# Running sums of squares for the next batch: accumulating DMAs in place of VectorE additions

## The chip, the cores and the metric

The kernel runs on one core of a Trainium2 chip. The metric is the device time of one execution in microseconds (us); the time of a kernel is the median of its runs. The engines of the core are TensorE (PE, matrix products; PEld is its loading of weights), VectorE (DVE), ScalarE (ACT), GpSimd (POOL), and SyncE (SP), which here only issues transfers. Each engine works through its own instructions in their order and waits on semaphores where it needs what another engine, or a transfer, has made.

## What is computed

Two layers follow one another: an attention between channels, for 4 batches of 6016 rows and 256 channels, and a gated feed-forward layer for all 24064 rows.

```python
# B, N, C = 4, 6016, 256; d_ff = 1536; float32 in and out
qn = q / (norm(q, axis=1) + 1e-6)          # norms over the 6016 rows, one for each channel
kn = k / (norm(k, axis=1) + 1e-6)
s  = kn.transpose(0, 2, 1) @ qn / tau      # 256 x 256 for each batch
a  = softmax(s)
x  = (v @ a).reshape(B * N, C)
out = (sigmoid(x @ w_gate) * (x @ w_val)) @ w_out
```

The norms need, for each batch, the sum over all rows of the squares of q and of k. Those sums are what the change touches.

## The kernel before

The kernel folds the attention of a batch into the two weights of the feed-forward layer (the tiles gh_G and gh_H), so that a batch then runs as 12 pieces of up to 512 rows, each with 12 steps over d_ff. A step ("slot") is one gate product, one value product, a tanh on ScalarE and a multiplication on VectorE; the output products of the piece before are strewn between them. 4 x 12 x 12 = 576 slots make up nearly all of the time. While batch b runs through its slots, the scores, squares and norms of batch b+1 are computed beside it, as side work tied to slots.

The pools whose sizes matter:

```python
qkpool = pool("qkpool", 5)      # q and k tiles
sqpool = pool("sqpool", 2)      # squares, two buffers for q and two for k
mpool = pool("mpool", 2)
opool = pool("opool", 2)        # output rows
psg = pool("psg", 2, space=PSUM)   # ps_gate
psv = pool("psv", 2, space=PSUM)   # ps_val
```

The sums of squares: ScalarE squares four rows of each partition at a time (128 partitions x 4 x 256), the squares are added into the accumulator acc (one for q, w = 0, and one for k, w = 1), two halvings on VectorE fold the four columns of acc into one, and TensorE sums over the partitions.

```python
def acc_square(b, g, w):
    t0, nt = groups[g]
    src = qk[b, t0][w]
    acc = st[b]["acc"][w]
    st[b]["sq", w] = squares(b, t0, nt, w, nc.scalar, acc if g == 0 else None)

def acc_add(b, g, w):
    t0, nt = groups[g]
    if g == 0:
        return
    acc = st[b]["acc"][w]
    nc.vector.tensor_tensor(
        out=acc[:, :nt, :], in0=acc[:, :nt, :], in1=st[b]["sq", w][:, :nt, :], op=ALU.add
    )

def acc_fold(b, w):
    acc = st[b]["acc"][w]
    for n in (2, 1):
        nc.vector.tensor_tensor(out=acc[:, :n, :], in0=acc[:, :n, :], in1=acc[:, n : 2 * n, :], op=ALU.add)
```

The slots at which this side work stands (FC is 12, groups has 12 entries, the last one with 3 rows of a partition instead of 4):

```python
first, last = (14 if b == 0 else 0), 8 * FC
for g, (t0, nt) in enumerate(groups):
    s0 = first + g * (last - first) // NCH
    # ... loads of q and k, score products
    for w in range(2):
        at(s0 + 1 + 4 * w, acc_square, n, g, w)
        slot = s0 + 3 + 4 * w
        at(slot + 2 if w == 0 and slot % FC == 8 else slot, acc_add, n, g, w)
# ...
s0 = 8 * FC + 2
at(s0 if b == 0 else s0 - 2, acc_fold, n, 0)
at(s0 + 1 if b == 0 else s0, acc_fold, n, 1)
at(s0 + 3, norms_mm, n)
```

One slot of the main work, and what GpSimd does for the output rows:

```python
def glu(b, ci, f, between=None):
    # ... PE: ps_gate and ps_val, two products each of 128x512
    nc.scalar.activation(out=g_sb[:, :n], in_=ps_gate[:, :n], func=ACT.Tanh, scale=0.5)
    nc.vector.scalar_tensor_tensor(
        out=hts[b, ci][:, f, :n], in0=g_sb[:, :n], scalar=1.0, in1=ps_val[:, :n],
        op0=ALU.add, op1=ALU.mult,
    )

def whole(p):
    o = out_tile(b, ci)
    nc.scalar.copy(o[:, p : p + half + 1 : half, :], states[p]["ps"].rearrange("p (t c) -> p t c", c=C))
    # ...
    add = nc.gpsimd.tensor_tensor
    add(out=ends, in0=ends, in1=states[p]["m"][:, 1:3, :], op=ALU.add)
    add(out=ends, in0=ends, in1=mids, op=ALU.subtract)
```

GpSimd also issues the loads of q, k and v, which turn float32 into bfloat16. Batch 0 has its squares summed in the opening stage by other lines, which the change does not touch.

Of the kernel before, what the change touches and what calls it, by code (L numbers as in the profile page):

```python
# [13 lines left out]
ALU = mybir.AluOpType  # L14
# [39 lines left out]
def kernel(  # L54
# [20 lines left out]
    nc = tc.nc  # L75
# [76 lines left out]
    t0, nt = groups0[0]  # L152
# [40 lines left out]
    for f0, nf in pieces:  # L193
        if f0 + nf == DFF:
            load_v(0, 1)
        for w, src in enumerate((moe_w_gate, moe_w_val)):
            nc.gpsimd.dma_start(
                out=w_sb[w][f0 // FG][:, :, ds(f0 % FG, nf)],
                in_=src.rearrange("(t p) f -> p t f", p=P)[:, :, ds(f0, nf)],
# [5 lines left out]
    for n in range(FC // TPC):  # L205
        w_f32[n] = f32pool.tile([P, TPC, C], FP32, tag="f32", name="w_f32")
        nc.gpsimd.dma_start(
            out=w_f32[n], in_=moe_w_out.rearrange("(t p) c -> p t c", p=P)[:, n * TPC : (n + 1) * TPC, :]
# [16 lines left out]
    st = {}  # L225
# [17 lines left out]
    def squares(b, t0, nt, which, engine, sq=None):  # L243
        src = qk[b, t0][which]
        if sq is None:
            sq = sqpool.tile([P, TPC, C], BF16, tag=f"sq{which}", name=f"sq{which}")
        if engine is nc.scalar:
            nc.scalar.activation(out=sq[:, :nt, :], in_=src[:, :nt, :], func=ACT.Square)  # L248
        else:
            engine.tensor_tensor(  # L250
                out=sq[:, :nt, :], in0=src[:, :nt, :], in1=src[:, :nt, :], op=ALU.mult
            )
        return sq
# [27 lines left out]
    def acc_add(b, g, w):  # L281
        t0, nt = groups[g]
        if g == 0:
            return
        acc = st[b]["acc"][w]
        nc.vector.tensor_tensor(  # L286
            out=acc[:, :nt, :], in0=acc[:, :nt, :], in1=st[b]["sq", w][:, :nt, :], op=ALU.add
        )

    def acc_fold(b, w):  # L290
        acc = st[b]["acc"][w]
# [405 lines left out]
    acc = st[0]["acc"]  # L697
    last0 = len(groups0) - 1
    adds, ends = [], []
    for g, (t0, nt) in enumerate(groups0):  # L700
# [5 lines left out]
        sq = [squares(0, t0, nt, w, engines[w], acc[w] if g == 0 else None) for w in range(2)]  # L706
        while adds:
            w, last_sq = adds.pop()
# [44 lines left out]
    def side_work(b):  # L753
# [24 lines left out]
        for g, (t0, nt) in enumerate(groups):  # L778
            s0 = first + g * (last - first) // NCH
            if b == 0:  # L780
                at(max(FC - 3, s0 - 12), load_qk, n, t0, nt)
            elif s0 >= 24:
                at(s0 - 24, load_qk, n, t0, nt)
            for u in range(nt):
                at(first + (t0 + u) * (last - first) // NT, score, n, t0, u)
            if g == 0:
                at(s0, acc_start, n)
# [4 lines that stand above are left out]
# [98 lines left out]
```

## Time and profile before

| What | Value |
|---|---|
| Time, median of 3 runs | 802.43 us (802.38 to 802.65) |
| Span of the profiled execution | 800.8 us |
| Granted TensorE clock | 0.998 of full speed |
| VectorE additions into acc (line 286) | 66, 58.9 us in all |
| Loads of v, 256 KB each, issue to landing | 5.2 us (median) |
| Share of the DMA engines' time, GpSimd's queue and SyncE's | 30.0% and 20.3% |

The profile has the busy time of each engine, the chain of waits that ended last, a row for each group of alike instructions (line, engine, operation, tiles, count, busy time, mean length, idle time before them and what ended it), and rows for transfers with the time from issue to landing. The time line of an engine gives, for each instruction, its start and its length in us, and in square brackets the idle time before it and what ended that. L128, L286 and so on are lines of the kernel.

### The profile page before, as it was taken

The numbers are of one execution on the slowest core, as the hardware profiler recorded it, in microseconds if no ns is written. First come the engines' busy times: TensorE is split into PE (matmuls) and PEld (weight loads), VectorE is DVE, ScalarE is ACT, GpSimd is POOL, SyncE is SP. The second block draws the span as 40 slices with busy tenths as digits, with TensorE's granted clock in tenths as the row PEclk, the third lists the DMA queues.
The fourth block names the chain that finished last, engine by engine and source line by source line (L and its number), as shares of the span: only waits on it lengthen the run. The fifth ranks groups of instructions, "written<-read, shape, count | busy, mean of one in ns | idle before, by whom it ended". The sixth has DMA issues, their size and how long they took to land.

```text
span 800.8 us, 17849 instructions
## 1 busy us (share of the span) xinstructions
PE 781.9 (98%) x6719; PEld 498.6 (62%) x6733; DVE 711.9 (89%) x1216; ACT 526.3 (66%) x887; POOL 359.8 (45%) x574
## 2 busy tenths in 40 slices
PE   4899999999999999999999999999999999999998
PEld 2556666666666666666666666666666566666666
DVE  5768999999979999999987999999998898998995
ACT  3766777765667777775667777776666566666664
POOL 4564545446443454335543544443544244444433
PEclk9999999999999999999999999999999999999999
DMA  9997757432765557422575477524323323423402
GB/s 214 205 194 132 132 98 139 89 67 53 139 120 105 93 114 128 85 53 55 111 127 106 96 124 119 99 54 93 66 55 87 66 54 78 82 54 77 76 28 74
DMA packets 79543, 78.89 MB, mean 99 GB/s; under 512 B 52064, under 2 KB 57312, under 8 KB 79456
## 3 DMA queue, kind: packets, MB, share of 16 engines
q0 software_dynamic: 22384, 39.60, 30.0%
q1 hardware_dynamic: 56496, 37.30, 20.3%
q8 instruction: 52, 0.85, 0.4%
q10 hardware_dynamic: 576, 0.85, 0.3%
q14 instruction: 35, 0.29, 0.1%
HBM read 79.04 MB, written 24.64 MB: 129 GB/s over the span
## 4 chain that ended last, share of the span: by engine, by line
PE 95%; DMA 3%; POOL 0%; issue 0%; DVE 0%; ACT 0%; POOLq 0%; DVEq 0%
PE ps_gate L128 30%; PE ps_val L128 30%; PE ps_o L128 28%; PE ps_s L128 4%; DMA k_sb<-in_k_dram 3%; PE ps_gh L128 2%; POOL q_sb L138 0%; PE ps_end L128 0%; POOL k_sb L138 0%; PE ps_n L128 0%; DVE x_sb L382 0%; PE ps_r L128 0%; ACT e_sb L400 0%; DVE y_sb L394 0%; POOL ident_f masks.py:199 0%
## 5 line engine op out<-in xcount | busy, mean ns | idle before, releaser
L520 ACT ACTIVATE g_sb<-ps_gate 128x512 f32<-128x512 f32 (+1 forms) x576 | 339.4, 590 | 224.7 <-PE ps_gate L128 213.9
L521 DVE SCALAR_TENSOR_TENSOR hT<-g_sb,ps_val 128x512 bf16<-128x512 f32 (+1 forms) x576 | 385.5, 671 | 70.0 <-ACT g_sb L520 59.5
L128 PE MATMUL ps_gate<-vT,gh_G 128*128 128x512 bf16 (+1 forms) x1152 | 337.6, 375 | 0.1
L128 PE MATMUL ps_val<-vT,gh_H 128*128 128x512 bf16 (+1 forms) x1152 | 337.5, 375 | 0.0
L543 DVE TENSOR_TENSOR sums<-hT 128x768 bf16<-128x768 bf16 (+1 forms) x460 | 282.0, 613 | 0.0
L128 PEld LDWEIGHTS <-sums 128*128 128x128 bf16 x2670 | 183.0, 98 | 81.9 <-DVE sums L543 0.5
L128 PEld LDWEIGHTS <-gh_H 128*128 128x128 bf16 x1152 | 112.7, 98 | 130.6 <-DVE gh_H L468 0.3
L614 POOL TENSOR_TENSOR out_sb<-out_sb,m_sb 128x256 f32<-128x256 f32 x89 | 78.2, 878 | 232.7 <-ACT out_sb L604 201.6
L128 PE MATMUL ps_o<-w_sums,sums 128*128 128x128 bf16 x1602 | 154.2, 219 | 0.0
L128 PEld LDWEIGHTS <-hT 128*128 128x128 bf16 x1200 | 88.3, 98 | 46.8
L598 POOL TENSOR_TENSOR m_sb<-m_sb 128x128 f32<-128x128 f32 x89 | 42.7, 479 | 149.9 <-ACT m_sb L597 149.8
L128 PEld LDWEIGHTS <-gh_G 128*128 128x128 bf16 x1152 | 96.6, 98 | 14.7 <-DVE gh_G L468 0.3
L128 PE MATMUL ps_o<-w_out_sb,sums 128*128 128x128 bf16 x1068 | 96.2, 219 | 0.0
L128 PE MATMUL ps_o<-w_sums,hT 128*128 128x128 bf16 x1068 | 95.5, 219 | 0.0
L128 PE MATMUL ps_s<-k_sb,q_sb 128*128 128x256 bf16 x376 | 70.5, 291 | 13.9 <-ACT k_sb L184 7.1
L615 POOL TENSOR_TENSOR out_sb<-out_sb 128x256 f32<-128x256 f32 x89 | 77.4, 870 | 7.0
L604 ACT COPY out_sb<-ps_o 128x512 f32<-128x512 f32 x89 | 52.3, 587 | 11.7 <-PE ps_o L128 9.4
L286 DVE TENSOR_TENSOR acc<-acc,sq 128x1024 bf16<-128x1024 bf16 (+1 forms) x66 | 58.9, 892 | 0.0
L599 POOL TENSOR_TENSOR m_sb<-m_sb 128x128 f32<-128x128 f32 x89 | 53.2, 598 | 7.0
L248 ACT ACTIVATE sq<-k_sb 128x1024 bf16<-128x1024 bf16 (+2 forms) x44 | 44.9, 1029 | 11.8 <-DMA k_sb<-in_k_dram 11.7
L128 PEld LDWEIGHTS <-q_sb 128*128 128x128 bf16 x376 | 33.5, 104 | 20.2 <-issue 9.5
L597 ACT COPY m_sb<-ps_o 128x384 f32<-128x384 f32 x89 | 42.7, 480 | 3.6 <-PE ps_o L128 1.0
(86 smaller groups left out, 306.6 us busy)
## 6 DMA issues: line engine op xcount, KB each, us to landing
out_dram<-out_sb SPq DMA_DIRECT2D x43, 512.0 KB, 3.4
v_sb<-in_v_dram POOLq DMA_DIRECT2D x44, 256.0 KB, 5.2
q_sb<-in_q_dram POOLq DMA_DIRECT2D x35, 256.0 KB, 4.4
k_sb<-in_k_dram POOLq DMA_DIRECT2D x35, 256.0 KB, 6.5
q_sb<-in_q_dram POOLq DMA_DIRECT2D x4, 512.0 KB, 11.6
k_sb<-in_k_dram POOLq DMA_DIRECT2D x4, 512.0 KB, 13.6
w_f<-in_moe_w_out_dram POOLq DMA_DIRECT2D x3, 512.0 KB, 9.4
out_dram<-out_sb SPq DMA_DIRECT2D x3, 384.0 KB, 2.8
```

What stands on the lines that cost most here:

```text
L128: nc.tensor.matmul(out, lhsT=lhsT, rhs=rhs, start=start, stop=stop, **kw)
L248: nc.scalar.activation(out=sq[:, :nt, :], in_=src[:, :nt, :], func=ACT.Square)
L286: nc.vector.tensor_tensor(out=acc[:, :nt, :], in0=acc[:, :nt, :], in1=st[b]["sq", w][:, :nt, :], op=ALU.add)
L520: nc.scalar.activation(out=g_sb[:, :n], in_=ps_gate[:, :n], func=ACT.Tanh, scale=0.5)
L521: nc.vector.scalar_tensor_tensor(out=hts[b, ci][:, f, :n], in0=g_sb[:, :n], scalar=1.0, in1=ps_val[:, :n], op0=ALU.add, op1=ALU.mult,)
L543: nc.vector.tensor_tensor(out=sums[b, ci, g][:, m, :, : half * P], in0=hT[:, f0 + k0 : f1 : 2, ds(r0 * half * P, half * P)], in1=hT[:, f0 ...
L597: nc.scalar.copy(m, states[p]["ps"][:, : 3 * P].rearrange("p (n c) -> p n c", c=P))
L598: nc.gpsimd.tensor_tensor(out=m[:, 1, :], in0=m[:, 1, :], in1=m[:, 2, :], op=ALU.add)
L599: nc.gpsimd.tensor_tensor(out=m[:, 2, :], in0=m[:, 1, :], in1=m[:, 0, :], op=ALU.add)
L604: nc.scalar.copy(o[:, p : p + half + 1 : half, :], states[p]["ps"].rearrange("p (t c) -> p t c", c=C),)
L614: add(out=ends, in0=ends, in1=states[p]["m"][:, 1:3, :], op=ALU.add)
L615: add(out=ends, in0=ends, in1=mids, op=ALU.subtract)
```

## The change

The additions of the squares into acc leave VectorE. Each becomes a transfer within the on-chip memory, issued from GpSimd's queue, which reads the squares and adds them into acc as it writes. The purpose is to take work off VectorE, which carries 89% of busy time. The fold, the squares and all slots stay as they are.

```diff
@@ acc_add
         if g == 0:
             return
         acc = st[b]["acc"][w]
-        nc.vector.tensor_tensor(
-            out=acc[:, :nt, :], in0=acc[:, :nt, :], in1=st[b]["sq", w][:, :nt, :], op=ALU.add
-        )
+        nc.gpsimd.dma_start(out=acc[:, :nt, :], in_=st[b]["sq", w][:, :nt, :], accum_op=ALU.add)
```

In the order of instructions that results, 66 additions go from VectorE and 66 transfers come to GpSimd's queue (22 for each of the batches 1, 2 and 3); no other instruction changes its place on any engine. Each transfer waits for its squares from ScalarE and for the transfer before it into the same accumulator, and the fold waits for the last of them.

## The prediction, made before the result was known

> **What bounds the kernel now.** I read the shares of busy time first, then the chain that ended last, then the rows of what the change touches.
>
> ```profile
> PE 781.9 (98%) x6719; PEld 498.6 (62%) x6733; DVE 711.9 (89%) x1216; ACT 526.3 (66%) x887; POOL 359.8 (45%) x574
> PE 95%; DMA 3%; POOL 0%; issue 0%; DVE 0%; ACT 0%; POOLq 0%; DVEq 0%
> L521 DVE SCALAR_TENSOR_TENSOR hT<-g_sb,ps_val 128x512 bf16<-128x512 f32 (+1 forms) x576 | 385.5, 671 | 70.0 <-ACT g_sb L520 59.5
> L286 DVE TENSOR_TENSOR acc<-acc,sq 128x1024 bf16<-128x1024 bf16 (+1 forms) x66 | 58.9, 892 | 0.0
> ```
>
> TensorE is busy for 98% of the span and is 95% of the chain; VectorE, which the change relieves, has 0% of the chain. Since a busy TensorE need not be one at its peak, I checked its rate. All its products together stream 1.807 million columns (the lengths of the moving operands summed over the trace). In the time line, back-to-back 128x512 products start every 0.215 us, so 512/0.215 = 2381 columns per us; 1.807 million at that pace is 759 us of the 800.8. The rest is nearly all in the opening: the list of waits has 13.9 us of TensorE waiting for the first q and k, all before the first slot. Adding up, from the starts of neighbouring products, what is over their columns gives 16.5 us in the first 40 us and then about 0.4 us in each 20 us, a little over 1 us only at the three changes of batch. The stretch table agrees (columns: stretch, its length, then PE, PEld, DVE, ACT, POOL busy with counts, clock, DMA share, GB/s):
>
> ```profile
> 340.00:360.00 20.00, 20.00 (x179) 12.88 (x177) 19.18 (x33) 14.43 (x25) 7.83 (x11) 1.00 0.25 53
> 660.00:680.00 20.00, 20.00 (x177) 12.49 (x176) 17.80 (x30) 11.99 (x22) 8.59 (x12) 1.00 0.31 71
> ```
>
> The first has side work, the second (last batch) has none. VectorE falls from 19.2 to 17.8, TensorE stays full in both. **There is almost nothing for a freer VectorE to win.** What can move the time is whether the change makes TensorE wait.
>
> [...] The trace shows GpSimd taking 0.57 us for a v load. [...] Here the smallest transfer from this queue (row<-rT, 0.5 KB) takes 2.7 us from issue to landing, so the measured 2.7 is used. [...] additions into acc take from 0.55 to 1.22 us, and the longer one shown below (1.08 us) lies beside GpSimd's additions. [...]
>
> **Part by part.**
>
> *Removed:* 66 x 0.892 = 58.9 us of VectorE, off the chain. Worth 0 to 1 us, from the rates above; I take 0.
>
> *Added on GpSimd:* 66 x 0.57 (the v load's) = 38 us; 45% busy becomes some 50%. Its waits are on ScalarE's copies (201.6 and 149.8 us in all), so this fits into its idle time.
>
> *Added on the DMA engines:* GpSimd's queue moved 22384 packets in 30.0% of 16 engines' span, so 0.30 x 16 x 800.8 / 22384 = 0.172 us for each. 66 x 128 rows = 8448 packets, at twice that (two reads, my choice) 8448 x 0.344 / 16 = 182 us, spread over some 490 us in which the engines are 25 to 60% busy. It fits.
>
> *The running chain:* a sum waits for the one before into the same acc. Squares of one w come 10.4 to 11.4 us apart (7.5 to 10.5 in batch 1). Landing in 5 to 7 us hides there.
>
> *The fold* is where the wait shows, for VectorE stands in the queue with main work behind it. Batch 2, on GpSimd, then on VectorE:
>
> ```profile
> 361.40 0.89 POOL L614 TENSOR_TENSOR out_sb<-out_sb,m_sb 128x256 f32<-128x256 f32 x1 [2.42 <-ACT out_sb L604]
> 362.36 0.93 POOL L615 TENSOR_TENSOR out_sb<-out_sb 128x256 f32<-128x256 f32 x1
> 363.23 0.57 POOL L148 DMA_DIRECT2D v_sb<-in_v_dram  x1
> ```
>
> ```profile
> 361.61 1.08 DVE L286 TENSOR_TENSOR acc<-acc,sq 128x768 bf16<-128x768 bf16 x1
> ...
> 365.54 0.75 DVE L293 TENSOR_TENSOR acc<-acc 128x512 bf16<-128x512 bf16 x2
> 366.20 0.68 DVE L521 SCALAR_TENSOR_TENSOR hT<-g_sb,ps_val 128x512 bf16<-128x512 f32 x1
> ```
>
> The last k addition (361.61) becomes a transfer. The new instruction order puts it on GpSimd behind the second pair of output additions, ahead of the v load: it is issued at 362.36 + 0.93 = 363.3, though its squares were ready at 358.5. The fold for k starts at 365.54, 2.2 us later. The hT behind it ends at 366.88, and the ps_val that reuses its bank starts on TensorE at 367.23:
>
> ```profile
> 367.23 0.59 PE L128 MATMUL ps_val<-vT,gh_H 128*128 128x512 bf16 x2
> ```
>
> 0.35 us of slack. **The landing time L** of this last transfer (three rows of 512 B in a partition, 192 KB) decides. Loads into 192 KB tiles land in 3.5 to 4.2 us, so 0.8 to 1.5 over the fixed 2.7. I double the 1.1 in the middle, since the accumulate reads two operands, and add 0.6 because a 512 KB output store is issued at 363.3 too: L = 2.7 + 2.2 + 0.6 = 5.5, an estimate. Landing at 368.8, fold to 369.5, hT to 370.1, TensorE late by 370.1 - 367.23 = 2.9.
>
> Batch 3 has the same pattern 192.7 us later: issue at 555.03 + 0.93 = 556.0, fold for k at 558.2, slack 0.36: late by 2.9. In batch 1 the slots differ by one, and the order puts the v load first: issue at 171.4, landing 176.9, where the fold began at 174.26 and the slack was 0.06: late by 2.4. The q folds are safe: issued at 166.1 (batch 1) against a fold at 172.2, and at 353.9 against 363.2.
>
> Sum: 2.4 + 2.9 + 2.9 = 8.2 us. Being full afterwards, TensorE never makes this up. 802.4 + 8.2 = 810.6; with half a us for stray delays, **811 us**.
>
> **Rivals.**
>
> 1. *Hidden anyway.* If the accumulate lands as a load does (L about 4.0), the delays are 0.9 + 1.4 + 1.4 = 3.7: about 806. For: no memory off the chip is touched. Against: the fixed 2.7 alone outlasts the 2.2 us between issue and fold, so nothing is hidden wholly.
> 2. *Slow accumulate.* If adding 16-bit elements runs at a quarter of a load's rate or less, L is 8 to 12. Each us of L costs 3 us: L = 8 gives about 819, L = 10 about 825. From about 10 us a second wait begins: the sums cannot keep pace with the squares, GpSimd stands blocked at its queue's head, output additions behind it come late, ScalarE's copies into m_sb and out_sb wait for buffers (two each), PSUM is not freed, and TensorE waits in every group of side work. That could reach 840 or more. The transfers would then also delay v loads. For: nothing in the profile has this rate. Against: nothing but that the casting loads keep 0.172 us a packet.
> 3. *VectorE was the bound.* It is 95% busy beside side work. If its additions held TensorE back, removing 58.9 us would bring some of it. Against: the full TensorE in both stretches, and the slack between hT and ps_val, which is small (0.06 to 1 us) but not negative.
>
> **Range and chances.** L from about 4 to 10 maps to 806 to 825; with stray gains and losses I give 804 to 826. 2% over 802.4 is 818.5, so an L of about 8.1. I put 0.29 on L beyond that or on a blocked queue, 0.01 on rival 3, and 0.70 on within 2%.
>
> **What would show it.** The row of additions at L286 gone from VectorE, its busy time down by 55 to 60 us, TensorE's nearly unchanged; a transfer row acc<-sq, x66, of 5 to 7 us to landing; among VectorE's waits a new one of the fold on that transfer, three times 2 to 4 us; new idle on TensorE just after each fold of k and nowhere else; the stretch between neighbouring folds as long as before (192.7 us) apart from it. The prediction is wrong if the span grows inside the groups before a fold (GpSimd blocked, rival 2), if GpSimd takes well over 0.57 us for an issue, if L is under 3.5 or over 9, or if the span shrinks.

## The result and the profile after

The changed kernel takes 809.17 us (median of 4 runs, 808.11 to 810.24) against 802.45 us before (median of 4 runs). The ratio is 1.0083, 95% interval 1.0065 to 1.0102: 6.7 us slower, within 2%, and close to the 811 predicted. The profiled execution has a span of 806.2 us against 800.8.

The page of the changed kernel: busy time by engine, the chain that ended last, then the main VectorE row, the row of the products into ps_val, the new row on GpSimd, and the new transfer with its median time from issue to landing.

```profile
PE 782.4 (97%) x6719; PEld 498.7 (62%) x6733; DVE 671.7 (83%) x1150; ACT 525.1 (65%) x887; POOL 415.7 (52%) x640
...
PE 92%; DMA 5%; POOL 1%; DVE 1%; issue 1%; ACT 0%; DVEq 0%; POOLq 0%
...
L519 DVE SCALAR_TENSOR_TENSOR hT<-g_sb,ps_val 128x512 bf16<-128x512 f32 (+1 forms) x576 | 387.8, 674 | 109.0 <-ACT g_sb L518 92.9
L128 PE MATMUL ps_val<-vT,gh_H 128*128 128x512 bf16 (+1 forms) x1152 | 337.5, 375 | 3.2 <-DVE hT L519 3.2
...
L286 POOL DMA_DIRECT2D acc<-sq x66 | 58.1, 881 | 6.5 <-ACT sq L248 1.9
...
acc<-sq POOLq DMA_DIRECT2D x60, 256.0 KB, 5.2
```

VectorE lost its row at L286 and 40 us of busy time; TensorE is as busy as before (782.4 against 781.9 us), in a longer span. What VectorE was spared turns up as its waiting for ScalarE: its idle time before hT grew from 70.0 to 109.0 us. The chain has larger shares for transfers (5%, from 3%) and for VectorE (1%, from 0%), and ps_val has 3.2 us of idle time that it did not have. Its row in the kernel before:

```profile
L128 PE MATMUL ps_val<-vT,gh_H 128*128 128x512 bf16 (+1 forms) x1152 | 337.5, 375 | 0.0
```

TensorE's list of waits in the changed kernel (who waited for whom, us in total, times, longest) says which:

```profile
PE ps_s L128 <- DMA k_sb<-in_k_dram: 6.9, 5, 2.1
PE ps_s L128 <- ACT k_sb L184: 6.9, 1, 6.9
PE ps_val L128 <- DVE hT L519: 3.2, 2, 1.6
PE ps_n L128 <- DVE acc L291: 2.3, 1, 2.3
```

The first two belong to the opening and were there before (6.8 and 7.1 us). The other three waits are new, 5.5 us together, which is the growth of the span (5.4). VectorE's list has their cause:

```profile
DVE acc L291 <- DMA acc<-sq: 7.2, 3, 2.8
```

Three folds of k, one for each of batches 1 to 3, wait for the last transfer into the accumulator. The time lines of batch 2 show one of them. GpSimd first, the instruction's start and length in us:

```profile
363.89 0.89 POOL L612 TENSOR_TENSOR out_sb<-out_sb,m_sb 128x256 f32<-128x256 f32 x1 [2.29 <-ACT out_sb L602]
364.86 0.73 POOL L613 TENSOR_TENSOR out_sb<-out_sb 128x256 f32<-128x256 f32 x1
365.53 0.86 POOL L286 DMA_DIRECT2D acc<-sq  x1
```

VectorE:

```profile
367.17 0.68 DVE L519 SCALAR_TENSOR_TENSOR hT<-g_sb,ps_val 128x512 bf16<-128x512 f32 x1
370.05 0.75 DVE L291 TENSOR_TENSOR acc<-acc 128x512 bf16<-128x512 bf16 x2 [2.20 <-DMA acc<-sq]
370.72 0.68 DVE L519 SCALAR_TENSOR_TENSOR hT<-g_sb,ps_val 128x512 bf16<-128x512 f32 x1
```

TensorE:

```profile
369.30 0.59 PE L128 MATMUL ps_gate<-vT,gh_G 128*128 128x512 bf16 x2
371.46 0.59 PE L128 MATMUL ps_val<-vT,gh_H 128*128 128x512 bf16 x2 [1.56 <-DVE hT L519]
```

The transfer is issued at 365.53, behind the output additions, and takes 4.4 us to land; the fold, ready since about 367.8, starts at 370.05; hT follows it at 370.72; TensorE, which needs the ps_val buffer that this hT reads, stands 1.56 us.

### The profile page after: what moved, and what is told of

Read it like the earlier page. It is cut to its first block, busy times and chain, and to the rows that moved or that the text cites. A ratio compares the mean times of both kernels' runs of the same rounds, so it can differ in the third digit from the quotient of the medians.

```text
span 806.2 us, 17947 instructions
## 1 busy us (share of the span) xinstructions
PE 782.4 (97%) x6719; PEld 498.7 (62%) x6733; DVE 671.7 (83%) x1150; ACT 525.1 (65%) x887; POOL 415.7 (52%) x640
## 3 DMA queue, kind: packets, MB, share of 16 engines
q0 software_dynamic: 31888, 56.51, 43.3%
## 4 chain that ended last, share of the span: by engine, by line
PE 92%; DMA 5%; POOL 1%; DVE 1%; issue 1%; ACT 0%; DVEq 0%; POOLq 0%
PE ps_val L128 29%; PE ps_gate L128 29%; PE ps_o L128 27%; PE ps_s L128 4%; DMA k_sb<-in_k_dram 3%; PE ps_gh L128 2%; DMA acc<-sq 2%; POOL out_sb L612 0%; ACT out_sb L602 0%; DVE acc L291 0%; POOL q_sb L138 0%; DVE hT L519 0%; PE ps_end L128 0%; POOL k_sb L138 0%; PE ps_n L128 0%
## 5 line engine op out<-in xcount | busy, mean ns | idle before, releaser
L519 DVE SCALAR_TENSOR_TENSOR hT<-g_sb,ps_val 128x512 bf16<-128x512 f32 (+1 forms) x576 | 387.8, 674 | 109.0 <-ACT g_sb L518 92.9
L541 DVE TENSOR_TENSOR sums<-hT 128x768 bf16<-128x768 bf16 (+1 forms) x460 | 285.7, 621 | 0.0
L612 POOL TENSOR_TENSOR out_sb<-out_sb,m_sb 128x256 f32<-128x256 f32 x89 | 83.9, 942 | 201.2 <-ACT out_sb L602 170.1
L596 POOL TENSOR_TENSOR m_sb<-m_sb 128x128 f32<-128x128 f32 x89 | 45.6, 513 | 123.1 <-ACT m_sb L595 122.9
L613 POOL TENSOR_TENSOR out_sb<-out_sb 128x256 f32<-128x256 f32 x89 | 67.4, 757 | 7.0
L286 POOL DMA_DIRECT2D acc<-sq x66 | 58.1, 881 | 6.5 <-ACT sq L248 1.9
L602 ACT COPY out_sb<-ps_o 128x512 f32<-128x512 f32 x89 | 52.1, 586 | 11.8 <-PE ps_o L128 9.5
L597 POOL TENSOR_TENSOR m_sb<-m_sb 128x128 f32<-128x128 f32 x89 | 54.7, 615 | 7.0
L248 ACT ACTIVATE sq<-k_sb 128x1024 bf16<-128x1024 bf16 (+2 forms) x44 | 44.8, 1027 | 12.0 <-DMA k_sb<-in_k_dram 11.8
```

The source lines that it names most:

```text
L286: nc.gpsimd.dma_start(out=acc[:, :nt, :], in_=st[b]["sq", w][:, :nt, :], accum_op=ALU.add)
L519: nc.vector.scalar_tensor_tensor(out=hts[b, ci][:, f, :n], in0=g_sb[:, :n], scalar=1.0, in1=ps_val[:, :n], op0=ALU.add, op1=ALU.mult,)
L541: nc.vector.tensor_tensor(out=sums[b, ci, g][:, m, :, : half * P], in0=hT[:, f0 + k0 : f1 : 2, ds(r0 * half * P, half * P)], in1=hT[:, f0 ...
L596: nc.gpsimd.tensor_tensor(out=m[:, 1, :], in0=m[:, 1, :], in1=m[:, 2, :], op=ALU.add)
L597: nc.gpsimd.tensor_tensor(out=m[:, 2, :], in0=m[:, 1, :], in1=m[:, 0, :], op=ALU.add)
```

## Experiments

The theory: the loss is three waits of the fold on the last k transfer of a batch, fixed by the distance between issue and fold; the other 63 transfers are hidden, and the relief of VectorE brings nothing. The rivals: the loss is spread over all 66 transfers (a longer GpSimd queue, traffic), or a gain from the relief hides inside it.

**Last group back on VectorE.**

```diff
+        if g == NCH - 1:
+            nc.vector.tensor_tensor(... acc + sq, as before ...)
+        else:
             nc.gpsimd.dma_start(..., accum_op=ALU.add)
```

> Undoes one part: only the additions of the last group (q and k, 6 in all) go back to VectorE, 60 of the 66 transfers stay. If the whole loss is the fold's wait for the last k transfer (my theory), TensorE no longer waits after the fold and the time is 802 to 803 us. If the loss is spread, by GpSimd's longer queue, by the transfers' traffic or by a lower clock, at least two thirds of it stay: 807 us or more.

Measured: 801.87 us (801.67 to 801.96), ratio to before 0.9993 (0.9984 to 1.0001). With 60 of the 66 transfers still in place, nothing of the loss is left.

**Only the last k addition as a transfer.**

```diff
+        if (g, w) != (NCH - 1, 1):
+            nc.vector.tensor_tensor(... acc + sq, as before ...)
+        else:
             nc.gpsimd.dma_start(..., accum_op=ALU.add)
```

> The mirror: only the last k addition of each batch (3 of 66) is an accumulating transfer, all others stay on VectorE. Theory: the loss is as large as with all 66, some 808 to 810 us. If the loss is spread over the 66 transfers: 803 us or less.

Measured: 809.8 us (808.89 to 810.82), ratio 1.0091 (1.0076 to 1.0106). Three transfers do what 66 do. VectorE's list of waits for this kernel has three waits of about the same sum (7.3 against 7.2 us), though not wait for wait (the longest is 3.4 us here, against 2.8):

```profile
DVE acc L296 <- DMA acc<-sq: 7.3, 3, 3.4
```

**The last k transfer earlier in GpSimd's queue.**

```diff
             for w in range(2):
                 at(s0 + 1 + 4 * w, acc_square, n, g, w)
                 slot = s0 + 3 + 4 * w
+                if (g, w) == (NCH - 1, 1):
+                    at(8 * FC - 2, acc_add, n, g, w)
+                    continue
```

> All 66 transfers stay, but the last k one is put one or two slots earlier in GpSimd's queue, so that it no longer stands behind the second pair of output additions (and, in batch 1, the v load). It can be issued when its squares are ready, some 4.3 us earlier in batches 2 and 3 and 3.5 us earlier in batch 1. Theory: it lands before the fold in batches 2 and 3 and about on time in batch 1, and the time is 802 to 803.5 us. If the wait is for GpSimd or for the number of transfers, the time stays at 807 or more.

Measured: 802.07 us (801.99 to 802.18), ratio 0.9995 (0.9987 to 1.0004). GpSimd's time line of this kernel has the transfer ahead of the second pair of output additions, instead of behind it:

```profile
358.88 0.86 POOL L286 DMA_DIRECT2D acc<-sq  x1
361.24 0.87 POOL L612 TENSOR_TENSOR out_sb<-out_sb,m_sb 128x256 f32<-128x256 f32 x1 [1.50 <-ACT out_sb L602]
```

VectorE's list of waits no longer has the fold. The transfer also lands faster: in 3.4, 3.0 and 3.6 us in batches 1 to 3, instead of 6.1, 4.4 and 4.5. It now runs ahead of the output store and the v load, which fits, but this run does not tell the two apart. All 66 transfers can be hidden, and then the kernel is as fast as before; that it is faster is not shown, since the interval has 1 in it.

**No additions at all.** The additions of groups 1 to 11 are left out; the norms of batches 1 to 3 are then those of the first group alone.

```diff
         if g == 0:
             return
         acc = st[b]["acc"][w]
-        nc.gpsimd.dma_start(out=acc[:, :nt, :], in_=st[b]["sq", w][:, :nt, :], accum_op=ALU.add)
+        return
```

> The additions of groups 1 to 11 are left out altogether (the norms of batches 1 to 3 then use the first group alone, so part of the computation is missing): VectorE has its 58.9 us less and nothing takes their place. Theory: TensorE was full already, so 802 to 802.5 us, the same as before within 0.1%. If VectorE had held TensorE back: 795 to 800 us.

Measured: 802.44 us, ratio 0.9999 (0.9990 to 1.0008). Taking the 58.9 us of additions from VectorE with nothing in their place is worth nothing, so the relief had nothing to give.

**The fold one slot later.**

```diff
-        at(s0 + 1 if b == 0 else s0, acc_fold, n, 1)
-        at(s0 + 3, norms_mm, n)
-        at(s0 + 4, root_seed, n)
-        at(s0 + 4, root_steps, n)
+        at(s0 + 2 if b == 0 else s0 + 1, acc_fold, n, 1)
+        at(s0 + 4, norms_mm, n)
+        at(s0 + 5, root_seed, n)
+        at(s0 + 5, root_steps, n)
```

> The changed kernel with the fold of k, the norm products and the start of the square root each one slot (1.25 us) later; the transfers stay as they are. Theory: each of the three delays gets shorter by the slot, 2.6 to 1.3 us in batch 1 and 1.7 to 0.45 us in batches 2 and 3, so 3.8 us less in all, some 804 to 806 us. If the delay didn't come from the distance between issue and fold: no change, 808 to 810 us.

Measured: 804.81 us (804.09 to 805.19), ratio 1.0028 (1.0018 to 1.0038). Its list for TensorE:

```profile
PE ps_n L128 <- DVE acc L291: 1.0, 1, 1.0
PE ps_val L128 <- DVE hT L519: 0.7, 2, 0.4
```

The delays fell from 2.3 to 1.0 us in batch 1 and from 1.6 to about 0.4 us in the other two: 5.5 to 1.7, which is 3.8 us, as the slot of 1.25 us foretold. Over this one slot, the delay is a distance, microsecond for microsecond (3.8 us for three times 1.25).

**The v load behind the last k transfer in batch 1.** Everywhere else this order already holds.

```diff
+                if b == 0 and (g, w) == (NCH - 1, 1):
+                    at(8 * FC - 1, acc_add, n, g, w)
+                    continue
```

> The changed kernel with one pair of instructions exchanged: in batch 1 the last k transfer is issued just ahead of the v load of 256 KB instead of just behind it, as batches 2 and 3 have it already. In the changed kernel this transfer took 6.1 us from issue to landing in batch 1, against 4.4 and 4.5 us in the other two. If the v load in front of it is the cause: it is issued 0.6 us earlier and lands 4.4 to 4.6 us later, VectorE's wait at that fold falls from 2.8 to about 0.6 us, and the time is about 807 us. If batch 1 is slower for another reason (more traffic in that stretch, the output store issued at the same moment): the landing stays near 6 us, the gain is the 0.6 us alone, and the time is about 808.6 us.

Measured: 806.82 us (806.2 to 807.12), ratio 1.0053 (1.0037 to 1.0070). The transfer is issued at 170.27 instead of 170.85 and lands after 5.0 us instead of 6.1; VectorE's wait there is 1.1 us, not the 0.6 expected. The load in front was most of what made batch 1 slower (1.1 of some 1.6 us); the remaining half a microsecond against 4.4 to 4.5 us is not explained by these runs.

**Copies in place of accumulations.** The squares overwrite acc and no sum is formed, so the norms of batches 1 to 3 come from the last values copied.

```diff
-        nc.gpsimd.dma_start(out=acc[:, :nt, :], in_=st[b]["sq", w][:, :nt, :], accum_op=ALU.add)
+        nc.gpsimd.dma_start(out=acc[:, :nt, :], in_=st[b]["sq", w][:, :nt, :])
```

> The 66 transfers stay where they are in the changed kernel, but copy the squares over acc and add nothing (so the running sum is left out and each norm comes from the last group). This tells what the adding itself costs. My prediction doubled the moving part of a 192 KB load for the second operand. If that is so, a plain copy of 256 KB lands well before the 5.2 us of the accumulate, at about 4 us, each of its packets takes about half of 0.18 us, and the issue on GpSimd falls from 0.88 to about 0.57 us; the time falls to about 806 us. If adding is free beside copying: the same 5 us, and 808 to 810 us.

Measured in one run: 806.07 us. The line of its transfers:

```profile
acc<-sq POOLq DMA_DIRECT2D x60, 256.0 KB, 4.0
```

TensorE's waits at the folds are these:

```profile
PE ps_n L128 <- DVE acc L291: 1.9, 1, 1.9
PE ps_val L128 <- DVE hT L519: 1.8, 2, 1.0
```

They come to 3.7 us, and the time is 3.6 us above that of the kernel before. Adding costs 1.2 us of landing time for 256 KB (5.2 against 4.0), 0.5 to 1.0 us for the three last k transfers (6.1, 4.4 and 4.5 against 5.6, 3.9 and 3.5), and the issue on GpSimd takes 0.88 against 0.57 us. It is the number of packets that grows, not the length of one, which I had expected to double. The changed kernel's queue has 31888 packets where the kernel before had 22384, so 9504 for the 66 transfers; with plain copies it has 27568, so 5184. From the queue's shares, (43.3% x 806.2 - 30.0% x 800.8) x 16 / 9504 = 0.18 us for an accumulating packet and (38.1% x 804.2 - 30.0% x 800.8) x 16 / 5184 = 0.20 us for a plain one; both are estimates, which take the other packets to be as long as before. In the trace a 256 KB accumulation is 128 packets of 2 KB and 16 of 4 bytes; of the 5184 packets of the plain copies 1056 are under 2 KB, 16 for each, and the rest comes to 64 of 4 KB for 256 KB.

**Every addition of groups 1 to 10 issued twice** (on the version with the early last issue; those groups then count twice in the norms).

```diff
-        nc.gpsimd.dma_start(out=acc[:, :nt, :], in_=st[b]["sq", w][:, :nt, :], accum_op=ALU.add)
+        for _ in range(2 if g < NCH - 1 else 1):
+            nc.gpsimd.dma_start(out=acc[:, :nt, :], in_=st[b]["sq", w][:, :nt, :], accum_op=ALU.add)
```

> Made from the version with the early last issue (802.1 us): each addition of groups 1 to 10 is issued twice in a row into the same accumulator (the sums are then wrong by a factor; 126 transfers in place of 66). The second of a pair must wait on GpSimd for the landing of the first, about 5 us in which GpSimd's queue stands, 60 times. It tells how far the hidden part is from its limit. If the queue has room (theory: squares come 10 us apart, two landings of 5.2 us just about fill this), output additions come up to 5 us late and their buffers absorb most of it: 802 to 812 us. If a standing queue blocks ScalarE's copies and with them TensorE (the second rival of the prediction): 1 to 4 us for each pair, 830 us or more.

Measured: 992.76 us (990.5 to 994.82), ratio 1.237 (1.2348 to 1.2393). The theory's 802 to 812 was far off; the rival's branch was right. The waits of this kernel, the longest first, with lines left out:

```profile
POOL acc L287 <- DMA acc<-sq: 255.0, 61, 8.5
...
ACT m_sb L596 <- POOL out_sb L613: 157.4, 27, 12.6
...
PE ps_o L128 <- ACT m_sb L596: 85.1, 16, 10.5
```

Read downwards it is the second rival of the prediction: GpSimd stands 61 times, 4.2 us on average, until the first of a pair has landed; ScalarE's copies into m_sb wait for GpSimd; TensorE waits for ScalarE. My error was to count one accumulator. Both stand in the same queue, so a group costs some 2 x (4.2 + 2 x 0.86) = 11.8 us of GpSimd, an estimate from this list and the 0.86 us of one issue in the time line, where squares came every 10.3 to 11.3 us in batch 2 of the kernel before, ahead of its other work. The added time, 190 us over 60 pairs, is 3.2 us for each. Not all of it is this chain: TensorE waited another 22.8 us where the folds stood for their last transfers, and some 51 us of the longer span are more time of TensorE outside its waits (989.8 less 152.5 us of waits, against 800.8 less 14.8), with the same products, at the lower clock that the last section shows.

## Why the prediction was right

*TensorE is full, the relief is worth nothing.* Shown: 802.44 us without any additions, 802.07 us with all of them hidden.

*The 63 other transfers are hidden.* Shown: 60 stay at no cost with the last group on VectorE, and the last k one alone costs as much as all 66. The q folds did not wait, as said. "It fits" was tighter than reckoned, though. The engines were called 25 to 60% busy; from the first transfer of a batch to its last (66.9 to 171, 252.4 to 365.5 and 445.8 to 560 us) the kernel before has a DMA share of 0.58, 0.52 and 0.54 (0.76 from 60 to 100 us), and the changed kernel 0.90, 0.87 and 0.83, with 1.01 from 100 to 160 us. One landing took 11.1 us, and GpSimd stood once, for 0.4 us, until the sum before had landed.

*Three waits at the k folds.* Shown. The size of the terms differs from the prediction's:

| Delay of TensorE, us | Predicted | Measured | Landing time, predicted 5.5 |
|---|---|---|---|
| Batch 1 | 2.4 | 2.3 | 6.1 |
| Batch 2 | 2.9 | 1.6 | 4.4 |
| Batch 3 | 2.9 | 1.6 | 4.5 |
| Sum | 8.2 | 5.5 | |

The working gave all three the same landing time. In batches 2 and 3 that was too long by 1.0 to 1.1 us, and its terms were off in both directions. Issued early, ahead of the store and the v load, the same transfers land in 3.0 and 3.6 us, so what comes on top of the 2.7 is 0.3 to 0.9 us and not 2.2; where they stand in the changed kernel they take 1.4 and 0.9 us more than that, and not 0.6. Nor is the 2.7 a floor for a transfer within the on-chip memory: it was read from row<-rT, which goes to memory off the chip, and the fastest plain copies, of 192 or 256 KB, land in 2.3 us in each of the three batches. The rest of the difference is slack: 0.64 us in batch 2 (the fold waits 2.20, TensorE 1.56) and not 0.35. In batch 1 the landing was 0.6 us longer than predicted: the v load in front, which cost 1.1 us by the exchanged pair, had been seen, but priced only as a later issue. An issue 0.6 us earlier than reckoned made up for it, so the 2.4 is right by two errors that cancel. (The figures printed there give 176.9 - 174.26 - 0.06 = 2.6; 2.4 takes a fold of 0.75 us in place of the 1.00, as it then was.) Batch 1's delay shows at ps_n, which waits for the fold directly, not at ps_val: the norm products stand only two slots after the fold, and the prediction had followed hT alone.

*The sum came close partly by luck.* The waits are 5.5 us where 8.2 were predicted, a third less; the medians differ by 6.7. The four runs of the changed kernel lie near 808.1 and near 810.2 us, with a mean granted clock of 0.998 to 1.000 in the two near 808.1 and 0.995 to 0.996 in the others. So about a microsecond of the median goes with the lower clock, a term that the prediction did not have; against the 808.1, its 811 is 2.9 us too long.

*Smaller terms.* GpSimd's issues took 58.1 us, not 38, because an accumulate is longer to issue (0.88 us) than a load of v (0.57 us) (the prediction names this among its signs of being wrong, and in this term it was). VectorE's busy time fell by 40.2 us, not 55 to 60: hT and the sums took 6.0 us more in all (387.8 against 385.5 us, 285.7 against 282.0), and neighbouring instructions overlap in the time line by about 0.1 us (the fold's 370.05 + 0.75 against the next start at 370.72), so that lengths add up to more than busy time; what is left of the difference was not traced. The packets, reckoned at 8448 of 0.344 us, were 9504 of some 0.18 by the estimate above, so 109 us on each of the 16 DMA engines instead of 182. The additions of 0.55 to 1.22 us that the prediction sets side by side are of two shapes: 0.55 to 1.08 us with 768 columns, 0.68 to 1.22 with 1024. One of 768 columns took 0.55 us too (at 169.78, beside GpSimd's addition at 169.83), so a link between the longer ones and GpSimd's additions is not shown.

*The rivals.* Hidden anyway: not so, but only for lack of 2 to 3 us. Slow accumulate: the doubled run shows that the mechanism is real (GpSimd stood 255.0 us there), at a load that this change does not reach. VectorE as the bound: excluded.

## What to carry to other kernels

Before relieving an engine, ask whether the one that bounds the kernel ever waits for it: 59 us off VectorE bought nothing, since TensorE waited for it in no slot (its list of waits in the kernel before has 0.2 us for VectorE, once, at ps_rk). When a short addition becomes a transfer, what counted here was the distance from its issue, with all that stands ahead in the issuing queue, to its first reader: moving one instruction by one or two slots was the difference between 809.2 and 802.1 us. A chain of transfers into one place can make its issuing queue stand for each landing (255.0 us in the doubled run), so every chain that shares the queue has to be added up before saying that it is hidden.

## What the runs showed that I had not expected

In the doubled run the granted clock was lower where TensorE stood. It averages 0.919. The table of stretches of that kernel (length, then PE, PEld, DVE, ACT, POOL busy with counts, clock, DMA share, GB/s) shows where:

```profile
100.00:160.00 60.00, 39.54 (x277) 23.39 (x277) 24.42 (x41) 20.40 (x34) 22.67 (x35) 0.87 0.71 120
...
800.00:900.00 100.00, 100.00 (x854) 61.73 (x852) 88.16 (x149) 60.40 (x107) 38.77 (x57) 1.00 0.32 70
```

With TensorE busy for 39.5 of 60 us the clock was 0.87; with TensorE full it was 1.00. The share alone does not set it: it was 0.89 from 420 to 440 us of this kernel, with TensorE busy for 17.9 of 20 us, and 1.00 from 162 to 180 us of the changed kernel, with TensorE busy for 15.7 of 18. Delays as short as those at the folds may go with it too: the kernels whose longest single delay after the opening is 2.3 us or more (the changed one, and the last k addition alone, 3.0 us) have four of eight runs with a clock of 0.995 to 0.996 and a time about 2 us longer. The kernels whose longest is 1.6 us (the exchanged pair in batch 1) or 1.0 us (the later fold) have none in 14 runs. No execution of these four kernels with the lower clock was profiled, so the link is a reading and is not shown.
